# Softmax sums of A in row layout, reciprocals spread by DMA through DRAM, products on GpSimd

## Chip, cores, metric

One core of a Trainium2 chip. The metric is the device time of one launch in microseconds (us), median of the executions named. The kernel before takes 271.1 to 274.1 us in all rounds of this study.

## The reference, cut to what matters

```python
def sm(a, b):                                  # softmax over the last axis
    s = scale * a @ b.T; e = exp(s - max(s)); return e / (sum(e) + 1e-9)
A  = sm(q, k_lm)          # 576 rows x 32 landmarks, per batch (8) and head (8)
Bm = sm(q_lm, k_lm); C = sm(q_lm, k)
Z  = six Newton steps for the inverse of Bm
x  = A @ Z @ C @ v                             # then, over 4608 rows:
out = (sigmoid(x @ w_gate) * (x @ w_val)) @ w_out
```

## The kernel before

The exponentials of A (`aexp`) lie transposed: 128 partitions are four heads times 32 landmarks, the columns are the 576 rows, for two groups of heads. To normalise, each column wants a sum over the 32 partitions of its head, and the reciprocal must go back to those 32 partitions. The kernel folds Z, C, v and the gate weights into U and V, so the gate matmuls read the normalised A (`an`) directly.

```python
def norm(b):                                        # before, every batch
    for n in range(NB):                             # 10 matmuls with 4 columns
        for g in range(2):
            mm(out=sm[:, n, g, :], lhsT=aexp[:, g, blk0[n]:blk0[n] + 128], rhs=blk[:, :, 0])
    dve.reciprocal(out=ra, in_=sm_ra[:, 0])
    ...                                             # split into two bf16 parts, rhl
    tr(out=rt_ps, in_=rhl..., identity=ident)       # one transpose
    dve.tensor_copy(out=rt, in_=rt_ps)
    for g in range(2):
        for w, ns in ((0, (0, 1, 2)), (1, (3, 4))):
            for n in ns:                            # 10 matmuls: spread over 32 partitions
                mm(out=rb[...], lhsT=sel[...], rhs=rt[...])
            dve.tensor_mul(out=an[:, g, n0:n0 + nn], in0=aexp[:, g, n0:n0 + nn], in1=rb)

def ffn1(b):                                        # the gate step of batch b
    yield need(u_at, v_at - 0.24, an, banks=2)
    for g in range(2): mm(out=gp, lhsT=U[:, g, js], rhs=an[:, g, ws])
    for g in range(2): mm(out=vp, lhsT=V[:, g, js], rhs=an[:, g, ws])

def front(b):                                       # landmarks of batch b, b >= 3
    ...                                             # k and q transposed by DMA, summed on GpSimd
    pool.tensor_add(out=klm, ...); pool.tensor_add(out=bq[...], ...)
    yield made(mid_of, b - 1)
    load(b + 1, "v")                                # on GpSimd's DMA queue
```

One thing must be known for the rest. The order of all instructions is laid out when the program is built, by a **model** of the engines inside the kernel. `need(...)` holds a stream back until the model thinks its data have landed; other streams, output matmuls (op) above all, fill the time. On the chip every engine then works its list in order. Where the chip is later than the model, the engine stands.

The softmax here doesn't subtract the row's maximum and nothing guards it: scores larger than these inputs give would overflow.

Of the kernel before, what the change touches and what calls it, by code (L numbers as in the profile page):

```python
# [7 lines left out]
FP32 = mybir.dt.float32  # L8
BF16 = mybir.dt.bfloat16
# [11 lines left out]
class Model:  # L21
# [113 lines left out]
    def swap(self, src, dst):  # L135
# [3 lines left out]
        end = max(self.free["sp"], self.free["dma"]) + 2.5  # L139
        self.used[src.name] = self.used[dst.name] = self.landed[dst.name] = end  # L140


class Timed:

# [33 lines left out]
def kernel(ctx, tc, q, k, v, moe_w_gate, moe_w_val, moe_w_out, out):  # L178
# [12 lines left out]
    nc = tc.nc  # L191

    B, H, S, D = q.shape
# [3 lines left out]
    HF = S // 2  # L197
    NP = H // 2
# [9 lines left out]
    blk0 = [0, 128, 256, 384, S - 128]  # L208
    ITERS = 6

    DEFER = {"bs": 1.0, "sl": 1.0, "sa": 3.0, "cv": 0.5, "up": 0.0}
    LEAD, FIRST, ORDER = 100.0, (2,), ('k2', 'q2', 'o0', 'o1', 'o2', 'v2', 'k3', 'q3', 'v3')

    TURN, LATE = 3, 2
# [1 line left out]

    SWAP = 3

    consts = ctx.enter_context(tc.tile_pool(name="consts", bufs=1))
    wpool = ctx.enter_context(tc.tile_pool(name="wpool", bufs=1))  # L220
    keep = ctx.enter_context(tc.tile_pool(name="keep", bufs=1))
    sb = ctx.enter_context(tc.tile_pool(name="sb", bufs=2))
    ps = ctx.enter_context(tc.tile_pool(name="ps", bufs=3, space=bass.MemoryType.PSUM))
    ctx.enter_context(tc.manual_schedule())

    BANKS = 8
    model = Model(BANKS)
    act = Timed(nc.scalar, "act", model)
    dve = Timed(nc.vector, "dve", model)
    pool = Timed(nc.gpsimd, "pool", model)  # L230

    def bank(shape, dtype, name, hold=False):

        return model.take(ps.tile(shape, dtype, name=name, tag="p", bufs=BANKS), hold)
# [4 lines left out]
    def mm(slow=0.0, **kw):  # L239
        rhs, lhsT = kw["rhs"], kw["lhsT"]  # L240
        n = 1
        for x in rhs.shape[1:]:
            n *= x
        c = 1
        for x in lhsT.shape[1:]:
            c *= x
        nc.tensor.matmul(**kw)  # L247
        at = [x.start_partition() if hasattr(x, "start_partition") else 0 for x in (lhsT, kw["out"])]
        return model.pe(kw["out"], [lhsT, rhs], lhsT.shape[0], c, n, tuple(at), slow)

    def tr(**kw):
        nc.tensor.transpose(**kw)  # L252
        return model.pe(kw["out"], [kw["in_"]], kw["in_"].shape[0], 128, kw["in_"].shape[0])

    def need(*data, banks=0, tile=None):


        return data, banks, None if tile is None else DEFER[tile]

# [32 lines left out]
    def load_out(fc):  # L292
# [11 lines left out]
        out=ident, in_=ident, compare_op=ALU.not_equal, fill=1.0,  # L304
# [13 lines left out]
    for p in range(3):  # L318
# [4 lines left out]
        out=perm, in_=ident[0:P6, 0:P6].rearrange("p (l r) -> p r l", r=3))  # L323
# [3 lines left out]
        out=seg3, in_=ident[0:P6, 0:P6].rearrange("p (l r) -> p l r", r=3), axis=AX.X, op=ALU.max)  # L327
# [3 lines left out]
        out=comb, in0=ident[:, None, 0:64].to_broadcast([128, 2, 64]),  # L331
        in1=ident[:, None, 64:128].to_broadcast([128, 2, 64]))
# [8 lines left out]
        out=sel0, in0=ident[0:2 * NR, 0:NR], in1=ident[0:2 * NR, NR:2 * NR])  # L341

    blk0_ = consts.tile([128, NP], BF16, name="blk0")
    nc.vector.tensor_reduce(
        out=blk0_, in_=ident.rearrange("p (i l) -> p i l", l=m), axis=AX.X, op=ALU.max)
# [7 lines left out]
    front_of, sums_of, lm_of, value_of, mid_of, norm_of, an_of, uv_of, step_at = ({} for _ in range(9))  # L353
# [155 lines left out]
    def mid(b):  # L509
# [7 lines left out]
        bs = bank([128, 2, m], FP32, f"bs_{b}")  # L517
        for g in range(2):
            for i in range(NP):
                mm(  # L520
                    out=bs[32 * i:32 * i + 32, g, :], lhsT=bq[0:64, 2 * i + g, 0:m],
                    rhs=klm[0:64, 2 * i + g, :], start=True, stop=True,
# [47 lines left out]
        if b == 0:  # L570
            cs = bank([128, 2], FP32, f"cs_{b}", True)
            cv = [bank([128, D], FP32, f"cv_{b}{g}", True) for g in range(2)]
# [79 lines left out]
        spread(bd, Bc)  # L652


        aexp = sb.tile([128, 2, S], BF16, name=f"aexp_{b}", tag="aexp", bufs=2)

        def a_scores(g):
            for c, x in enumerate(row_scores("sa", g, klm, 0, qT)):
# [30 lines left out]
        if 0 < b < TURN:  # L689
            yield need(*cexp_at.values(), v_landed[0], banks=2)  # L690
            cs = bank([128, 2], FP32, f"cs_{b}")
            cv = bank([128, 2, D], FP32, f"cv_{b}")
            cv = [cv[:, g] for g in range(2)]
# [21 lines left out]
        if b >= TURN:  # L715
            value_of[b] = late_value

    def norm(b):

        aexp = norm_of.pop(b)  # L720
        yield need(aexp, banks=1)

        sm_ra = bank([128, 2, NR], FP32, f"sm_{b}")
        sm = sm_ra[:, 0].rearrange("p (n g i) -> p n g i", n=NB, g=2)
        for n in range(NB):
            for g in range(2):
                mm(
                    out=sm[:, n, g, :], lhsT=aexp[:, g, blk0[n]:blk0[n] + 128], rhs=blk[:, :, 0],
                    start=True, stop=True)
        ra = sm_ra[:, 1]  # L730
        dve.reciprocal(out=ra, in_=sm_ra[:, 0])
        rhl = sb.tile([128, 2, NR], BF16, name=f"rhl_{b}", tag="rhl")
        dve.tensor_copy(out=rhl[:, 0, :], in_=ra)
        dve.tensor_sub(out=rhl[:, 1, :], in0=ra, in1=rhl[:, 0, :])
        yield need(rhl, banks=1)
        rt_ps = bank([2 * NR, 128], BF16, f"rtp_{b}")
        tr(out=rt_ps, in_=rhl.rearrange("p s r -> p (s r)"), identity=ident)
        rt = sb.tile([2 * NR, 128], BF16, name=f"rt_{b}", tag="rt")
        dve.tensor_copy(out=rt, in_=rt_ps)
        an = sb.tile([128, 2, S], BF16, name=f"an_{b}", tag="an", bufs=3)  # L740
        for g in range(2):
            for w, ns in ((0, (0, 1, 2)), (1, (3, 4))):
                yield need(rt, banks=1)
                n0 = 384 * w
                nn = min(S, n0 + 384) - n0
                rb = bank([128, nn], FP32, f"rb_{b}_{g}{w}")
                for n in ns:
                    lo = 64 if n == 4 else 0
                    o = blk0[n] + lo - n0
                    mm(  # L750
                        out=rb[:, o:o + 128 - lo],
                        lhsT=sel[:, (2 * n + g) * NP:(2 * n + g + 1) * NP, :],
                        rhs=rt[:, lo:128], start=(n == ns[0]), stop=(n == ns[-1]))
                dve.tensor_mul(
                    out=an[:, g, n0:n0 + nn], in0=aexp[:, g, n0:n0 + nn], in1=rb)
        an_of[b] = an
# [15 lines left out]
    def advance_by(b, g, out, lhs, rhs, name, twice=False):  # L772

        p = bank([128, rhs.shape[1]], FP32, name)
        mm(out=p, lhsT=minus2, rhs=rhs, start=True, stop=False)
        mm(out=p, lhsT=lhs, rhs=rhs, start=False, stop=True)
        return each(b, g).mul(out, p[:, None, :].to_broadcast([128, 2, D]) if twice else p, -1.0)

    def first_newton(b):
        y, bd, at = mid_of[b]  # L780
        y = y[:, :, 128:128 + D]
        for it in range(ITERS):
            last = it == ITERS - 1
            n = sb.tile([128, 2, 2, D] if last else [128, 2, D], BF16, name=f"y_{b}_{it + 1}", tag=f"y{last}", bufs=2)
            model.by_part.add(n.name)
            new = []
            for g in range(2):
                yield lambda: 0.0 if len(square_of[b]) > it else None
                S, s_at = square_of[b][it]
                yield need(at[g], s_at[g], banks=1)  # L790
                new.append(advance_by(b, g, n[:, g], S[:, g, 0:128], y[:, g], f"py_{b}_{it}{g}", last))
            y, at = n, new
        return y, at
# [215 lines left out]
    def mids():  # L1009
        for b in range(B):  # L1010
            yield made(lm_of, b)
            if b > 2:
                yield step(b - 2)
            yield from mid(b)

    def norms():
        for b in range(B):
            yield made(norm_of, b)
            yield from norm(b)
# [126 lines left out]
```

## Time and profile before

| | before |
|---|---|
| median of 3 | 271.84 us |
| span of the profile | 269.7 us |
| TensorE, VectorE, ScalarE, GpSimd busy | 260.1, 193.3, 159.4, 96.2 us |
| TensorE clock granted | 0.998 |

The span runs from the first to the last instruction and stands about 2 us under the time. TensorE is the engine that bounds; the lines are in the prediction. Here is what the prediction doesn't show and the argument needs: SyncE's queue, the one that carries output, transposes and small exchanges, in the timeline of the kernel before (start, length, queue, line, operation, out<-in, count).

```profile
138.25 1.12 SPq L480 DMA_DIRECT2D s_5q<-s_5q  x2
144.38 0.79 SPq L959 DMA_DIRECT2D out_dram<-ob  x2
149.04 1.33 SPq L384 DMA_TRANSPOSE ct<-cl  x1
```

It is busy here and there, in order, and nothing in it is waited for by the gate step.

### The profile page before, as it was taken

The numbers are of one execution on the slowest core, as the hardware profiler recorded it, in microseconds if no ns is written. First come the engines' busy times: TensorE is split into PE (matmuls) and PEld (weight loads), VectorE is DVE, ScalarE is ACT, GpSimd is POOL, SyncE is SP. The second block draws the span as 40 slices with busy tenths as digits, with TensorE's granted clock in tenths as the row PEclk, the third lists the DMA queues.
The fourth block names the chain that finished last, engine by engine and source line by source line (L and its number), as shares of the span: only waits on it lengthen the run. The fifth ranks groups of instructions, "written<-read, shape, count | busy, mean of one in ns | idle before, by whom it ended". The sixth has DMA issues, their size and how long they took to land.

```text
span 269.7 us, 8019 instructions
## 1 busy us (share of the span) xinstructions
PE 260.1 (96%) x3089; PEld 167.0 (62%) x3123; DVE 193.3 (72%) x551; ACT 159.4 (59%) x413; POOL 96.2 (36%) x107
## 2 busy tenths in 40 slices
PE   8999999999999999999999999999999999999994
PEld 5877777757664666556646665556636664665443
DVE  4566888976899788948986778848968786963111
ACT  3663876866647754876477655875368643964001
POOL 8523231960874039511953078212922000000000
PEclk9999999999999999999999999999999999999999
DMA  6999999999795998889794989589530413101433
GB/s 94 193 206 205 205 206 206 205 203 172 141 194 115 204 170 121 181 135 199 141 221 72 182 157 203 129 139 199 124 90 12 97 41 80 41 0 41 117 103 92
DMA packets 62645, 38.00 MB, mean 141 GB/s; under 512 B 33552, under 2 KB 58128, under 8 KB 62608
## 3 DMA queue, kind: packets, MB, share of 16 engines
q0 software_dynamic: 23600, 18.88, 47.0%
q1 hardware_dynamic: 38896, 18.52, 31.4%
q8 instruction: 24, 0.39, 0.6%
q14 instruction: 13, 0.11, 0.1%
q10 hardware_dynamic: 112, 0.10, 0.1%
HBM read 37.75 MB, written 9.44 MB: 175 GB/s over the span
## 4 chain that ended last, share of the span: by engine, by line
PE 93%; ACT 2%; issue 2%; POOL 1%; DVE 0%; POOLq 0%; ACTq 0%
PE op L247 34%; PE gp L247 18%; PE vp L247 18%; PE idle_ps L247 3%; PE pn L247 2%; PE cv L247 2%; PE rb L247 2%; PE sc L247 1%; PE sa L247 1%; PE tp_q L252 1%; PE up_1g L247 1%; PE up_0g L247 1%; PE up_2g L247 1%; PE tp_k L252 1%; PE up_1v L247 1%
## 5 line engine op out<-in xcount | busy, mean ns | idle before, releaser
L247 PE MATMUL op<-wo_sb,ht 128*128 128x512 bf16 (+1 forms) x410 | 109.4, 373 | 2.1 <-issue 1.1
L153 ACT ACTIVATE th<-gp 128x288 bf16<-128x288 f32 x192 | 76.7, 415 | 48.4 <-PE gp L247 36.7
L153 DVE SCALAR_TENSOR_TENSOR ht<-th,vp 128x288 bf16<-128x288 bf16 x192 | 82.0, 448 | 21.9 <-ACT th L153 17.2
L247 PE MATMUL gp<-an,U 128*128 128x288 bf16 x384 | 78.5, 286 | 0.3
L247 PE MATMUL vp<-an,V 128*128 128x288 bf16 x384 | 78.4, 286 | 0.0
L247 PEld LDWEIGHTS <-ht 128*128 128x128 bf16 x444 | 39.9, 98 | 26.7 <-issue 5.8
L247 PEld LDWEIGHTS <-U 128*128 128x128 bf16 x384 | 35.9, 98 | 27.3 <-issue 2.5
L247 PEld LDWEIGHTS <-V 128*128 128x128 bf16 x384 | 37.5, 98 | 9.7 <-issue 0.2
L153 ACT ACTIVATE ob<-op 128x512 f32<-128x512 f32 (+1 forms) x31 | 18.2, 587 | 29.6 <-PE op L247 24.2
L153 DVE SCALAR_TENSOR_TENSOR sy<-sy,pn 128x384 bf16<-128x384 bf16 x35 | 19.2, 548 | 2.3 <-PE pn L247 1.9
L153 DVE TENSOR_SCALAR ob<-op 128x512 f32<-128x512 f32 (+2 forms) x7 | 4.2, 596 | 17.3 <-PE op L247 17.3
L247 PE MATMUL idle_ps<-idle_w 128*128 128x256 bf16 x86 | 14.8, 308 | 1.2 <-DVE idle_w L297 1.2
L247 PE MATMUL pn<-sy 128*128 128x192 bf16 (+1 forms) x84 | 13.1, 237 | 0.4 <-ACT kT L153 0.3
L153 DVE TENSOR_TENSOR an<-aexp,rb 128x384 bf16<-128x384 bf16 (+1 forms) x32 | 12.4, 446 | 0.3 <-PE rb L247 0.3
L247 PEld LDWEIGHTS <-sy 128*128 128x128 bf16 x88 | 8.1, 97 | 6.2 <-DVE sy L153 2.8
L153 ACT ACTIVATE aexp<-sa 128x288 bf16<-128x288 f32 x32 | 10.7, 418 | 1.5 <-PE sa L247 1.1
L247 PEld LDWEIGHTS <-idle_w 128*128 128x128 bf16 x86 | 8.5, 109 | 3.3 <-DVE idle_w L297 1.2
L247 PEld LDWEIGHTS <-WT 64*32 64x32 bf16 x384 | 3.8, 89 | 9.1 <-issue 6.6
L270 POOL DMA_DIRECT2D kn<-in_k_dram x9 | 7.0, 779 | 4.6 <-DMA wg_sb<-in_moe_w_gate_dram 2.1
L153 DVE CAST U<-up_0g 128x512 bf16<-128x512 f32 x8 | 5.5, 690 | 4.1 <-PE up_0g L247 4.1
L270 POOL DMA_DIRECT2D vn<-in_v_dram x8 | 6.3, 789 | 5.3 <-PE gp L247 4.5
L270 POOL DMA_DIRECT2D qn<-in_q_dram x9 | 6.8, 753 | 4.0 <-PE sm L247 2.2
(201 smaller groups left out, 349.7 us busy)
## 6 DMA issues: line engine op xcount, KB each, us to landing
vn<-in_v_dram POOLq DMA_DIRECT2D x8, 576.0 KB, 9.4
kn<-in_k_dram POOLq DMA_DIRECT2D x7, 576.0 KB, 8.1
qn<-in_q_dram POOLq DMA_DIRECT2D x7, 576.0 KB, 10.6
out_dram<-ob SPq DMA_DIRECT2D x53, 64.0 KB, 3.0
out_dram<-ob SPq DMA_DIRECT2D x17, 192.0 KB, 2.3
out_dram<-ob SPq DMA_DIRECT2D x18, 128.0 KB, 2.4
wg_sb<-in_moe_w_gate_dram POOLq DMA_DIRECT2D x3, 512.0 KB, 19.7
wv_sb<-in_moe_w_val_dram POOLq DMA_DIRECT2D x3, 512.0 KB, 21.0
```

The lines of the kernel that those rows point to most:

```text
L153: f(**kw)
L247: nc.tensor.matmul(**kw)
L252: nc.tensor.transpose(**kw)
L270: nc.gpsimd.dma_start(out=t[:, hs], in_=src[b, hs].rearrange("h (p c) d -> p h (c d)", p=P6))
```

## The change

The intent: take the 21 small matmuls of the normalisation off TensorE and the products off VectorE. The sums come out in row layout (8 matmuls on 128x32 tiles), the reciprocals go out to DRAM and come back spread over 32 partitions each, and GpSimd, which idles, multiplies in place. Batches 2 to 7. Cut to its core:

```diff
+    def widen(self, src, dst, n=1):                 # what the model assumes of such a transfer
+        start = max(self.free["pe"], self.free["sp"], self.landed.get(src.name, 0.0), ...)
+        self.free["sp"] = start + 0.55 * n
+        self.free["dma"] = max(self.free["dma"], start) + 0.5 * n
+        end = max(self.free["dma"], self.free["sp"]) + 2.0
...
-        aexp = sb.tile([128, 2, S], BF16, name=f"aexp_{b}", tag="aexp", bufs=2)
+        aexp = sb.tile([128, 2, S], BF16, name=f"aexp_{b}", tag="aexp", bufs=3)
...
+    def wide_norm(b, aexp):
+        for c in range(2):
+            for j in range(4):
+                mm(out=sm[32 * j:32 * j + 32, :], lhsT=pairs[0][:, c], rhs=aexp[:, j // 2, o:o + QT], ...)
+        for x in range(2):
+            at = dve.reciprocal(out=ra[:, half], in_=sm[:, half])
+        far = away.tile([2, 2, NP, 4, HF], FP32, ...)               # in DRAM
+        nc.sync.dma_start(out=far..., in_=ra)
+        model.widen(ra, far)
+        yield need(far)
+        for i in range(NP):
+            nc.sync.dma_start(out=wide[32 * i:32 * i + 32], in_=far[:, :, i, 0]....partition_broadcast(32))
+        model.widen(far, wide, NP)
+        for j in range(4):
+            yield need(wide)
+            part = aexp[:, j // 2, (j % 2) * HF:(j % 2 + 1) * HF]
+            pool.tensor_mul(out=part, in0=part, in1=wide[:, j])
+        an_of[b] = aexp
...
-        an = sb.tile([128, 2, S], BF16, name=f"an_{b}", tag="an", bufs=3)
+        an = aexp                                                    # batches 0 and 1, old way, in place
```

More of the change, by code (lines that the diff above doesn't have):

```diff
@@ L140, in swap @@
         self.used[src.name] = self.used[dst.name] = self.landed[dst.name] = end
+    def widen(self, src, dst, n=1):
+        start = max(self.free["pe"], self.free["sp"], self.landed.get(src.name, 0.0),
+                    self.waits.get(dst.name, 0.0))
+        self.free["sp"] = start + 0.55 * n
+        self.free["dma"] = max(self.free["dma"], start) + 0.5 * n
+        end = max(self.free["dma"], self.free["sp"]) + 2.0
+        self.used[src.name] = self.used[dst.name] = self.landed[dst.name] = end
 class Timed:
@@ L209 @@
     ITERS = 6
-    DEFER = {"bs": 1.0, "sl": 1.0, "sa": 3.0, "cv": 0.5, "up": 0.0}
+    DEFER = {"bs": 1.0, "sl": 1.0, "sa": 3.0, "cv": 0.5, "up": 0.0, "sm": 1.0}
     LEAD, FIRST, ORDER = 100.0, (2,), ('k2', 'q2', 'o0', 'o1', 'o2', 'v2', 'k3', 'q3', 'v3')
@@ L217 @@
     SWAP = 3
+    WIDE, QT, pairs = 2, S // 4, []
     consts = ctx.enter_context(tc.tile_pool(name="consts", bufs=1))
@@ L222 @@
     sb = ctx.enter_context(tc.tile_pool(name="sb", bufs=2))
+    away = ctx.enter_context(tc.tile_pool(name="away", bufs=1, space=bass.MemoryType.DRAM))
     ps = ctx.enter_context(tc.tile_pool(name="ps", bufs=3, space=bass.MemoryType.PSUM))
@@ L716, in mid @@
             value_of[b] = late_value
+    def wide_norm(b, aexp):
+        if b == WIDE:
+            pairs.append(consts.tile([128, 2, 32], BF16, name="pairs"))
+            nc.vector.memset(pairs[0], 0.0)
+            to = pairs[0].rearrange("p c (i u d) -> p c i u d", u=4, d=2)
+            for c in range(2):
+                dve.tensor_copy(out=to[:, c, :, :, c], in_=blk0_[:, :, None].to_broadcast([128, NP, 4]))
+        yield need(aexp, banks=1, tile='sm')
+        sm = bank([128, QT], FP32, f"sm_{b}")
+        for c in range(2):
+            for j in range(4):
+                o = (j % 2) * HF + c * QT
+                mm(
+                    out=sm[32 * j:32 * j + 32, :], lhsT=pairs[0][:, c],
+                    rhs=aexp[:, j // 2, o:o + QT], start=(c == 0), stop=(c == 1))
+        ra = sb.tile([128, QT], FP32, name=f"ra_{b}", tag="ra", bufs=1)
+        for x in range(2):
+            half = slice(x * QT // 2, (x + 1) * QT // 2)
+            at = dve.reciprocal(out=ra[:, half], in_=sm[:, half])
+            yield need(at + (0.3 if x == 0 else 0.0))
+        far = away.tile([2, 2, NP, 4, HF], FP32, name=f"far_{b}", tag="far", bufs=2)
+        nc.sync.dma_start(out=far.rearrange("g w i u (c x) -> (g w i u c) x", c=2), in_=ra)
+        model.widen(ra, far)
+        yield need(far)
+        wide = sb.tile([128, 4, HF], FP32, name=f"rw_{b}", tag="rw", bufs=1)
+        for i in range(NP):
+            nc.sync.dma_start(
+                out=wide[32 * i:32 * i + 32],
+                in_=far[:, :, i, 0].rearrange("g w x -> (g w) x").partition_broadcast(32))
+        model.widen(far, wide, NP)
[4 more added lines that the diff above has]
+        an_of[b] = aexp
     def norm(b):
         aexp = norm_of.pop(b)
+        if b >= WIDE:
+            yield from wide_norm(b, aexp)
+            return
         yield need(aexp, banks=1)
@@ L783, in first_newton @@
             last = it == ITERS - 1
-            n = sb.tile([128, 2, 2, D] if last else [128, 2, D], BF16, name=f"y_{b}_{it + 1}", tag=f"y{last}", bufs=2)
+            n = sb.tile([128, 2, 2, D] if last else [128, 2, D], BF16, name=f"y_{b}_{it + 1}", tag=f"y{last}", bufs=1 if last else 2)
             model.by_part.add(n.name)
```

## The prediction

> **What bounds the kernel now.** I read the page first, then the busy time of each engine by stretch, then the chain of work that ended last, then the groups and tiles that the change touches, and last the timeline of GpSimd and of the SyncE queue.
>
> From the page of the kernel before, busy times, slices and the chain:
>
> ```profile
> PE 260.1 (96%) x3089; PEld 167.0 (62%) x3123; DVE 193.3 (72%) x551; ACT 159.4 (59%) x413; POOL 96.2 (36%) x107
> PE   8999999999999999999999999999999999999994
> PE 93%; ACT 2%; issue 2%; POOL 1%; DVE 0%; POOLq 0%; ACTq 0%
> ```
>
> TensorE is busy 96% of the span, and the chain that ended last runs through it for 93%. From 34 to 246 us the table by stretch says how little is left over (columns: window, length, then busy time of PE, weight load, VectorE, ScalarE, GpSimd, then clock, DMA share, GB/s):
>
> ```profile
> 34.00:246.00 212.00, 209.05 (x2377) 132.18 (x2407) 167.95 (x460) 136.45 (x357) 81.42 (x83) 1.00 0.78 140
> ```
>
> 212.00 - 209.05 = 2.95 us of TensorE idle time in that stretch. So what this change can give is TensorE time that it takes away, plus at most those 3 us.
>
> What the softmax normalisation of A costs TensorE is read from the chain of work between 126.5 and 132.5 us, batch 4 (start, length, what):
>
> ```profile
> 127.47 0.17 PE pn L247 x2
> 127.63 0.25 PE sm L247 x10
> 127.88 0.45 PE op L247 x2
> ...
> 128.99 0.43 PE op L247 x2
> 129.42 0.06 PE rtp L252
> 129.47 0.24 PE gp L247 x2
> ...
> 130.56 0.52 PE rb L247 x10
> 131.07 0.43 PE op L247 x2
> ```
>
> Everything is packed end to end, so these lengths are what the next instruction waited: 0.25 us for ten sums, 0.06 for one transpose, 0.52 for ten broadcasts of the reciprocals, 0.83 us a batch. The durations of single instructions (0.17 to 0.23 us) overlap and must not be summed. VectorE's share is in the groups:
>
> ```profile
> L153 DVE TENSOR_TENSOR an<-aexp,rb 128x384 bf16<-128x384 bf16 (+1 forms) x32 | 12.4, 446 | 0.3 <-PE rb L247 0.3
> L153 DVE RECIPROCAL sm<-sm 128x40 f32<-128x40 f32 x8 | 3.3, 409 | 0.0
> L153 POOL TENSOR_TENSOR s_5k<-kT 128x768 f32<-128x768 bf16 x1 | 1.6, 1643 | 11.3 <-DMA kT<-kn 11.3
> ```
>
> The third line is GpSimd: it waited 11.3 us for the transposed k of batch 5 at 126.92 us, then its timeline is full of landmark sums until 144 us. The normalisation of batch 4 falls exactly there.
>
> **What the Trainium skill says.** "TensorEngine Tiling (Array Packing)", Key Properties: tiles work in parallel, but changing the tiling mode drains the array. The trace agrees: 16 score matmuls (sa, 64x32 tiles, two rounds of 288 columns, 0.24 us at 2.4 columns per ns) hold the chain 0.37 us, so 0.13 us for the change, and a gap of 0.16 us follows at 126.44. "GPSIMD Engine Reference", Elementwise: a two-input operation takes about 2.6 cycles an element at 1.2 GHz; 768 elements took 1.643 us here, 2.57 cycles, so it agrees. "DMA: Bandwidth & Descriptors", Anatomy of one DMA: about 2 us of fixed cost, mostly waiting for the write receipt. The 64 KB exchanges of batch 7, with no loads about, land in 2.0 us; those of batches 3 to 6 for k, beside loads, in 5.6 to 6.2. So agreement on an empty queue only. "SBUF — State Buffer", Who interferes with whom: VectorE operations with two SBUF inputs hold up GpSimd's reads. The gate (th, vp) and the Newton step have one input in PSUM; the gate takes 396 to 455 ns all through the run, with GpSimd busy or not, so I expect little of this.
>
> **The change part by part**, for one batch of the six (2 to 7).
>
> TensorE, removed: 0.25 + 0.06 + 0.52 = 0.83 us. Added: eight matmuls of 128x32 tiles with 144 columns, four side by side, two rounds: 2 x 144 / 2.4 = 0.12 us, plus 0.13 to 0.29 us for the change of mode in and out (from sa above), less where the scheduler sets it beside other tiled work. I take 0.30. Net 0.53 us, all on the bounding engine: 6 x 0.53 = 3.2 us.
>
> VectorE, removed: reciprocal 0.41, two halves of the bf16 split 2 x 0.20, copy of the transpose 0.21, four products 4 x 0.446 = 1.78; sum 2.80 us. Added: two reciprocals of 72 columns. From 166 ns for 2 columns and 409 for 40, 6.4 ns a column: 0.166 + 70 x 0.0064 = 0.61 us each, 1.22 us. Net 1.6 us a batch, 9.5 us in all, but VectorE has 44 us to spare in the 212: beside other work. It can shorten only TensorE's waits on it, which are some 5 us of weight-load waits and under 3 us of idle. I count 0.3 us.
>
> GpSimd, added: four products of 288 elements at 2.57 cycles, 0.62 plus some 0.05 us each: 2.7 us a batch, 16 us in all, on an engine idle 64% of the time. Beside other work if its place in the queue is right.
>
> DMA, added: 73 KB out to DRAM, then four reads that write 147 KB each: 0.66 MB a batch, 4 MB on 38. It is not bandwidth but latency that counts. Before: first sum at 127.47, last product done at 132.76, 5.3 us. After: 0.3 for the matmuls, 0.2 to VectorE, 1.2 reciprocals, 2.5 to 5.5 for the write, 3 to 6 for the reads, 2.7 for the products: 10 us on an empty queue, 16 beside loads. The step that uses it, the first gate matmul of batch 4, comes 0.4 us after the last up matmul (139.9 us), 12.8 us after the first sum. So in batches 3 to 6 that step moves by up to 3 us, some more if the schedule, which is laid out from a model that puts a transfer behind all loads queued, thinks it later.
>
> Does that cost? Not at once: TensorE has other work. At the start of the eight gate steps I counted output matmuls (op) done against those whose input exists: at batches 3 to 6 some 55 to 64 are in reserve, 12 to 14 us at 0.216 us each. They fill a late step; batch 7, which ends the run, has no loads beside it (10 to 11 us, in time).
>
> Sum: 269.7 - 3.2 - 0.3 = 266.2 us of span; I give back 0.6 us for stalls where the schedule's guess of a landing is wrong. 266.8 of span, and the measured time stands 2.1 us above the span (271.84 against 269.7): 268.9 us, 1.1% faster.
>
> **The rivals.** First, **GpSimd's order**. The chain that paces the batches is: k transposed by DMA, GpSimd sums (126.92 to 144.3), landmark scores, softmax of C, its transpose (149.04), next k transposed (150.47, landed 156.6): 29.7 us a round, and the later gate steps start right when their weights are up (230.25 and 230.58). If the four products sit in GpSimd's queue before the landmark products bq (142.81), each round grows by 2.7 us or by the wait for the read as well. Five rounds: 14 us, of which the reserve hides some 8: about +5 us, so 274 to 275. For it: in-order queue, busy window. Against it: all sums of the next batch are issued before the products, and the reads land late enough to fall behind bq, where GpSimd idles over 10 us. Chance 0.15.
>
> Second, **a late operand becomes a TensorE stall**: writing, then reading through DRAM takes longer than the schedule thinks, and TensorE, in order, stands. One microsecond for each of five batches takes away 5 us: 271 to 274. For it: the spread of 2.0 to 6.2 us for the same exchange. Against it: the products come 10 us before most uses of that data end, and a schedule that assumes FIFO behind loads errs on the safe side. Chance 0.2.
>
> Third, **VectorE relief counts**: with six fewer PSUM banks asked for and 1.6 us less VectorE work a batch, most of the 3 us of idle goes too: 266 us. Chance 0.1.
>
> **Range and chances.** The main line gives 268 to 270; the third rival sets the low end, 266.2, the second the high end, 273.0. More than 2% faster means below 266.4, which needs all of the 0.83 us saved with nothing added, or the third rival in full: 0.08. More than 2% slower means above 277.3, the first rival beyond my estimate: 0.06. The rest, 0.86, is within 2%.
>
> **What would show it.** Right: sm, rtp and rb for batches 2 to 7 replaced by eight matmuls that hold the chain 0.25 to 0.4 us; TensorE busy near 257 us; VectorE down by about 9 us; GpSimd up by about 16; products ending 10 to 16 us after the sums; GpSimd's sums of the next k still 29 to 30 us apart; output matmuls moved ahead of the gate steps of batches 3 to 6. Wrong: TensorE idle between 34 and 246 us clearly above 3 us, with gate matmuls waiting for GpSimd; bq waiting behind the products; or output transfers held in the SyncE queue behind a read that waits for its write, with ScalarE waiting for its output buffers. The last matters as well if it lengthens the chain of k.

## The result

| | before | after |
|---|---|---|
| first chip, median of 4 | 272.16 us | 283.51 us (279.09 to 290.68) |
| ratio of fast runs, 95% interval | 1 | 1.028 (1.022 to 1.035) |
| another chip, 4 runs (again) | 272.91 us | 290.60 us; ratio 1.062 |
| a third set, 6 runs (again2) | 272.01 us | 288.63 us; ratio 1.054 |
| TensorE clock of the runs | 0.991 to 1.0 | 0.958 to 0.994 |

A ratio is the mean time of one kernel's fast runs over that of the other's of the same rounds, so not quite the ratio of the medians. Outputs are correct. The change is 3 to 6% slower, and it is unsteady: its executions differ by up to 4%. "Fast" is said within one call: the two fast runs of the first chip took 279.09 and 280.63 us at a clock of 0.994 and 0.992, while all four of again have 0.958 to 0.970 and would have counted as slow beside them. Those two faster executions were not profiled. The first profile of the change fell in the slow state, so I read the one of the run again, a fast one of its call. From its page, the busy times, slices of TensorE, and the clock, in tenths:

```profile
PE 265.7 (92%) x3014; PEld 164.7 (57%) x3046; DVE 189.6 (66%) x521; ACT 159.7 (55%) x410; POOL 112.9 (39%) x131
PE   8899999999966999999995899976999999989994
PEclk9999999999999799999999599996999999999999
```

TensorE has fewer instructions, yet is busy 5.6 us longer, in a span of 289.2 us; and the slices fall to 5 or 6 tenths where they were 9. The clock falls in or just after those slices. Who TensorE waits for is in its view of waits (us in total, times, longest):

```profile
PE gp L259 <- POOL aexp L162: 11.7, 7, 3.2
```

The chain of work in batch 4 shows one such stop whole (start, length, what):

```profile
132.55 0.13 PE sm L259 x8
132.68 0.35 PE gp L259 x2
...
145.81 0.22 PE up_2v L259 x8
146.02 0.35 PE gp L259 x2
...
149.47 0.42 SPq L757
...
150.91 7.16 DMA rw<-far
...
158.93 1.43 POOL aexp L162 x2
160.40 0.40 PE gp L259
160.79 0.48 PE vp L259 x2
161.27 0.21 PE s L259 x2
161.49 0.48 PE gp L259 x2
```

Three things are to be seen. The new sums cost TensorE 0.13 us, less than I thought. The reads of the reciprocals are issued at 149.47, 17 us after the sums, and one of them takes 7.16 us of the chain; the gate step, whose weight matmuls end at 146.03, starts its first matmul at 159.02, after a stop of 3.17 us, and its second at 160.4, after 1.10 us more. And from then on two gate matmuls take 0.48 us where they took 0.24: the clock is half. The Trainium skill, "TensorE: Matmul & The Clock Gate" (Part 1, What's actually happening), gives 1.2 GHz as the state "after ≥1 idle window (~3.4µs)". The case agrees on the half clock (granted 0.5), but not on a whole idle window: in batch 2 it fell to half behind stops of 1.48 and 1.10 us with a matmul between them. Three such stretches, behind batches 2, 4 and 5, last 3.4, 6.8 and 6.8 us, 17.1 us in all. Before the stop TensorE did have other work, as I had counted on, but it was used up. SyncE's queue and GpSimd in the same stretch:

```profile
137.01 0.54 SPq L752 DMA_DIRECT2D far<-ra  x1
144.76 1.11 SPq L492 DMA_DIRECT2D s_5q<-s_5q  x2
148.63 0.79 SPq L1011 DMA_DIRECT2D out_dram<-ob  x2
149.47 1.88 SPq L757 DMA_DIRECT2D rw<-far  x4
```
```profile
149.92 0.79 POOL L282 DMA_DIRECT2D vn<-in_v_dram  x1
158.23 2.80 POOL L162 TENSOR_TENSOR aexp<-aexp,rw 128x288 bf16<-128x288 bf16 x4 [7.52 <-DMA rw<-far]
```

The write lands in under 6 us (4.7 in batch 4), but the reads are issued 12.5 us after its issue, and the next v (576 KB) is loaded beside them. The reads stand in SyncE's queue behind an output transfer (148.63) that itself waited for its tile. All six batches of that run, from the same views (us; a read's time is from its issue to its landing):

| batch | sums | reads issued | v load issued | reads land in | first product | TensorE stops |
|---|---|---|---|---|---|---|
| 2 | 73.3 | 85.6 | 86.4 | 2.6 to 4.4 | 91.6 | 1.5 + 1.1 |
| 3 | 104.5 | 117.8 | 120.2 | 2.7 to 3.1 | 122.7 | none |
| 4 | 132.4 | 149.5 | 149.9 | 3.0 to 7.2 | 158.2 | 3.2 + 1.1 |
| 5 | 169.3 | 186.1 | 185.8 | 6.4 to 7.7 | 195.4 | 2.9 + 1.1 |
| 6 | 206.7 | 214.7 | none | 3.1 to 3.6 | 219.9 | none |
| 7 | 239.3 | 246.0 | none | 3.0 to 3.7 | 251.9 | 0.9 |

The kernel's own model can be printed while the order is laid out; for batch 4 of the changed kernel it believes:

```
sums 124.36   write landed 139.94   reads issued 140.02   reads landed 144.22
products done 147.41   gate step 147.51      end of the program: 261.23 (kernel before: 263.94)
```

From the sums on, the model issues the reads at +15.7 and ends the products at +23.1; the chip issues them at +17.1 and ends the products at 161.0, +28.7. The model's end of the program is 2.7 us earlier than that of the kernel before: it made the same forecast as I did, from the same error.

### The profile page after: what moved, and what is told of

Its sections match the earlier page's. It is cut to its first block, busy times and chain, and to the rows that moved or that the text cites. A ratio compares the mean times of both kernels' runs of the same rounds, so it can differ in the third digit from the quotient of the medians.

```text
span 288.8 us, 7934 instructions
## 1 busy us (share of the span) xinstructions
PE 265.0 (92%) x3014; PEld 163.8 (57%) x3046; DVE 188.2 (65%) x521; ACT 160.0 (55%) x410; POOL 112.8 (39%) x131
## 4 chain that ended last, share of the span: by engine, by line
PE 75%; DMA 11%; SPq 3%; POOL 3%; issue 3%; ACT 2%; DVE 1%; POOLq 1%; ACTq 0%; DVEq 0%
PE op L259 24%; PE gp L259 17%; PE vp L259 16%; DMA rw<-far 7%; PE idle_ps L259 2%; PE pn L259 2%; DMA s_3k<-s_3k 2%; POOL aexp L162 2%; DMA kn<-in_k_dram 2%; SPq L1011 2%; PE cv L259 2%; SPq L757 1%; PE sc L259 1%; PE sa L259 1%; PE tp_q L264 1%
## 5 line engine op out<-in xcount | busy, mean ns | idle before, releaser
L259 PE MATMUL op<-wo_sb,ht 128*128 128x512 bf16 (+1 forms) x412 | 104.1, 377 | 2.0 <-issue 1.2
L259 PE MATMUL gp<-aexp,U 128*128 128x288 bf16 x384 | 81.7, 294 | 12.8 <-POOL aexp L162 12.3
L259 PE MATMUL vp<-aexp,V 128*128 128x288 bf16 x384 | 80.8, 293 | 0.0
L259 PEld LDWEIGHTS <-ht 128*128 128x128 bf16 x444 | 40.8, 98 | 38.7 <-issue 7.9
L259 PEld LDWEIGHTS <-V 128*128 128x128 bf16 x384 | 38.4, 100 | 15.6 <-issue 4.9
L162 POOL TENSOR_TENSOR aexp<-aexp,rw 128x288 bf16<-128x288 bf16 x24 | 16.8, 730 | 61.8 <-DMA rw<-far 32.7
L162 ACT ACTIVATE ob<-op 128x512 f32<-128x512 f32 (+1 forms) x27 | 15.8, 586 | 32.8 <-PE op L259 29.2
L162 DVE TENSOR_SCALAR ob<-op 128x512 f32<-128x512 f32 (+2 forms) x11 | 6.9, 631 | 32.6 <-PE op L259 30.3
L162 DVE TENSOR_SCALAR sy<-s,rc 128x128 bf16<-128x128 f32 x15 | 4.6, 345 | 10.0 <-PE s L259 9.7
L162 ACT ACTIVATE cl<-sl 128x288 bf16<-128x288 f32 x20 | 8.0, 411 | 1.8 <-PE sl L259 1.7
```

The lines of the kernel that those rows point to most:

```text
L162: f(**kw)
L259: nc.tensor.matmul(**kw)
```

## The experiments

**Theory L**, after seeing the profile: the operand is late, TensorE stops, its clock falls. **Rivals**: G, the place of the products on GpSimd delays the landmark sums and so the pace of the batches; B, in-place work and the buffer counts; T, the traffic by itself.

### again: the changed kernel once more

No edit.

> The changed kernel once more, on the chip of the next three runs. Theory L (late operand: the reciprocals come back from DRAM about 5 us after the schedule expects them, TensorE stands at the first gate matmul, and its clock falls after the stop): 279 to 291 us, TensorE idle several us ahead of the first gate matmul of most of batches 2 to 7, released by the GpSimd products. Theory G (order on GpSimd: the four products delay the landmark sums, so each round of the chain that paces the batches grows): the same time. Theory B (working in place, three buffers for the exponentials): the same time.

290.60 us, ratio 1.062 (1.055 to 1.068). It is the profile read above.

### notrip: no transfers, constant reciprocals

Wrong on purpose, though by little, as the sums of 32 small exponentials are all near 32.

```diff
-        far = ...; nc.sync.dma_start(out=far..., in_=ra); yield need(far)
-        wide = ...; four reads
-            yield need(wide)
-            pool.tensor_mul(out=part, in0=part, in1=wide[:, j])
+            yield need(ra)
+            pool.tensor_mul(out=part, in0=part, in1=flat)     # a tile of 1/32
```

> Wrong on purpose: the products take a constant 1/32 instead of the reciprocals, and the two transfers are gone; sums, reciprocals and the four GpSimd products stay. L: no late operand, so the saved TensorE time shows: 0.70 us a batch as the chain has it (0.83 less 0.13), 4.2 us in all, 267 to 269 us, no stop of TensorE above 1 us after batch 1. G: the products still stand in the GpSimd queue, still 276 us or more. B: still 276 us or more.

270.92 us, ratio 0.994 (0.989 to 0.999). From its page:

```profile
PE 257.9 (96%) x3014; PEld 161.9 (60%) x3046; DVE 187.8 (70%) x518; ACT 160.4 (60%) x414; POOL 112.7 (42%) x131
PE   8999999999997999999999999999999999999994
PEclk9999999999999999999999999999999999999999
```

Same instructions on TensorE (3014), same products on GpSimd (112.7 us busy), and both the stops at the gate step and the clock loss are gone. With the wait for the transfers goes 19.7 us of time against again, which includes what the low clock took there. G and B predicted 276 us or more and fall. For G this is a hard test: without the wait the products of batch 4 stand at 138.81 in GpSimd's queue, ahead of klm and bq, the very place that the first rival feared. But 270.9 is above my 267 to 269.

### unread: the transfers made, but nobody waits

```diff
-            yield need(wide)
-            pool.tensor_mul(out=part, in0=part, in1=wide[:, j])
+            yield need(ra)
+            pool.tensor_mul(out=part, in0=part, in1=flat)
```

> Wrong on purpose: as the run before, but both transfers are made as in the changed kernel, into a tile that nobody reads. It asks what the traffic and the place in the SyncE queue cost by themselves. L: at most 1 us more than without the transfers, 267 to 270 us. A rival, theory T (the 4 MB more of traffic, or the SyncE queue held up, slows the transposes and the output): 273 us or more, with a longer time from the issue of the k transposes to their landing, or ScalarE and VectorE waiting for output buffers.

272.01 us, ratio 0.995 (0.990 to 1.000). From its page:

```profile
PE 258.2 (96%) x3014; PEld 162.2 (60%) x3046; DVE 189.5 (70%) x518; ACT 160.3 (59%) x414; POOL 112.7 (42%) x131
```

It is 1.1 us more than without the transfers, within the noise: so little the traffic and the places in SyncE's queue cost when nobody waits. T falls. In this run as in notrip the order laid out changes too, since the model no longer holds the gate step back: the difference to again is that of the whole late operand, planned wait and unplanned stop together. Against this page TensorE in again is 7.5 us longer busy (265.7), with the same instructions. My figure of at most 270 was missed by 2 us, by the same amount as the run before.

### wide8: old normalisation, new buffers

```diff
-    WIDE, QT, pairs = 2, S // 4, []
+    WIDE, QT, pairs = 8, S // 4, []
```

> The old normalisation in all eight batches, but in place and with the buffer counts of the changed kernel. L, G and T: as before, 271 to 273 us. B: 276 us or more.

274.53 us, ratio 1.005 (1.000 to 1.010). So the buffers (one of them, for the last Newton step, went from two to one) and the order that follows from them cost half a per cent, hardly clear of noise. That would explain the two misses above: against this run, which differs from notrip in the normalisation and the order laid out for it, the saving is 274.53 - 270.92 = 3.6 us, for the 4.2 us expected.

### told5: the model is told that the reads land later

```diff
-        end = max(self.free["dma"], self.free["sp"]) + 2.0
+        end = max(self.free["dma"], self.free["sp"]) + (7.0 if n > 1 else 2.0)
```

> The kernel's work unchanged, but the model from which its order is laid out is told that the reads land 5 us later, which is what the trace shows. My prediction's claim was that other matmuls fill a late step, some 12 us of them in reserve. If so, TensorE gets other work in place of the stops: 272 to 278 us. If the reserve is too small (the model itself ends 24 us later then, at 285 against 261), the time is as bad as the changed kernel or worse: 285 to 295 us.

293.99 us, ratio 1.082 (1.077 to 1.087). Knowing of the delay doesn't hide it. The model, printed in the same way, itself stood for 4.5, 5.3 and 2.1 us from 97.8 on, with 9 output tiles done of the 9 whose input existed: the reserve was empty. On the chip the order came out worse still. GpSimd's timeline:

```profile
107.95 1.48 POOL L162 TENSOR_TENSOR s_4q<-s_4q 128x256 f32<-128x256 f32 x2
109.39 2.81 POOL L162 TENSOR_TENSOR aexp<-aexp,rw 128x288 bf16<-128x288 bf16 x4
```

Those are the products of batch 2, whose reads were issued at 84.5: they got behind the whole block of landmark sums, and TensorE stood 7.4 us for them. So the run mixes an empty reserve with rival G, which the changed kernel itself doesn't show.

### vlate: the load of v after the products

```diff
                 yield made(mid_of, b - 1)
+                yield made(normed, b - 1)        # set once the products of b - 1 are in the queue
                 load(b + 1, "v")
```

> The load of the next v, which the changed kernel puts into the DMA queues just ahead of or beside the four reads of the reciprocals, is issued after the products instead. In the profile of the run again the reads landed in 2.7 to 3.1 us in batch 3 (v issued after them) and 3.5 in batch 6 (no v), and in up to 7.2 and 6.4 to 7.7 us in batches 4 and 5 (v just ahead). Theory V (that load makes the read late): reads of batches 4 and 5 land within 3.5 us, the stops there, 4.3 and 4.0 us, shrink to under 1 us, and with the half clock after them gone the time falls by 8 to 11 us, to 278 to 282. Rival (the wait is the round trip itself and the order in the SyncE queue): reads stay at 5 us or more, time as the changed kernel, 286 to 292.

279.11 us, ratio 1.026 (1.021 to 1.030): as expected, 11.5 us less than again. That difference holds both the shorter stops and the clock, which in this profile never falls to half after the start. It is also measured against a call of slow-clocked executions: the two fast runs of the unchanged program on the first chip, 279.09 and 280.63 us, are no slower than vlate. Each view of the reads below is of one batch, 4 and then 5, first of again and then of vlate:

```profile
DMA to landing us min/median/max: 3.0/4.2/7.2
DMA to landing us min/median/max: 6.4/7.1/7.7
```
```profile
DMA to landing us min/median/max: 2.8/3.1/3.3
DMA to landing us min/median/max: 3.1/3.4/3.6
```

The products of batch 4 begin 4.9 us after the first read is issued instead of 8.8:

```profile
149.44 1.84 SPq L758 DMA_DIRECT2D rw<-far  x4
154.31 2.81 POOL L162 TENSOR_TENSOR aexp<-aexp,rw 128x288 bf16<-128x288 bf16 x4 [2.48 <-DMA rw<-far]
```

The Trainium skill, "DMA: Bandwidth & Descriptors", Issuing engines are not separate DMA queues, says that transfers from all queues run on the same 16 DMA engines and interleave. This pair of runs agrees and adds the size: a 144 KB read lands in 2.7 to 3.6 us, and in up to 7.7 with one 576 KB load issued just before or among the reads. Stops of 1.1 to 1.9 us are left in four batches.

### warm: dummy matmuls over the stops

```diff
             gp = bank([128, HF], FP32, f"gp_{b}_{j}{w}")
+            for _ in range({2: 30, 4: 40, 5: 40, 7: 14}.get(b, 0) if w == 0 and j == 0 else 0):
+                nc.tensor.matmul(out=gp[:, 0:256], lhsT=idle_w[:, 0:128], rhs=idle_w, start=True, stop=True)
```

> The changed kernel with dummy matmuls (256 columns, into the bank of the first gate matmul, which overwrites them) ahead of the first gate matmul of batches 2, 4, 5 and 7: 30, 40, 40 and 14, 0.107 us each, about as long as the stops. The operand is as late as ever; only the clock is kept up. Theory C (much of the loss is the half clock that follows a stop: TensorE busy 265.7 us in the run again against 258.2 with unread transfers, 7.5 us): the time falls by 5 to 8 us, to 282 to 286, with the clock at 0.99 or above. Rival (the stop alone costs): no change or, where dummies outlast the stop, a longer time: 289 to 293.

287.78 us, ratio 1.056 (1.048 to 1.064), the clock 0.992 to 1.0 in all four runs. TensorE's timeline at batch 4:

```profile
155.63 4.53 PE L948 MATMUL gp<-idle_w 128*128 128x256 bf16 x40
160.00 0.29 PE L259 MATMUL gp<-aexp,U 128*128 128x288 bf16 x1
160.74 0.28 PE L259 MATMUL gp<-aexp,U 128*128 128x288 bf16 x1 [0.46 <-POOL aexp L162]
160.86 0.41 PE L259 MATMUL vp<-aexp,V 128*128 128x288 bf16 x2
```

The operand comes no sooner (160.7 against 160.4), the clock stays up, and the time, 2.8 us under again (an earlier call on the same chip), falls by less than the intervals. So filling the stops keeps the clock up, and in this pair the low clock isn't most of the loss. Theory C's 5 to 8 us aren't there.

### again2 and warm2: the same pair in one call, five rounds

warm2 has 52 dummies at batch 2 instead of 30.

> The changed kernel, beside the next two runs. 280 to 292 us, clock 0.96 to 0.99.

> The changed kernel with dummy matmuls over the stops, 52 in place of 30 at batch 2 (its stop there was 2.5 us longer than the dummies). The operand is as late as ever. Theory C (the half clock after a stop is a cost of its own): the clock stays at 0.99 or above, and the time is 3 to 8 us under the changed kernel of the same rounds. Rival (only the stop costs, or the half clock falls into waits that are there anyway): within 1.5 us of it.

again2: 288.63 us, ratio 1.054 (1.050 to 1.058). warm2: 288.15 us, ratio 1.061 (1.057 to 1.065), clock 0.993 to 1.0. No gain, though warm2's dummies outlast the stops in this execution (at batch 2 they run until 97.5, the products are there at 92.3), so what a full clock gives and what the dummies take can't be parted. How much of the loss is the half clock stays open. An upper bound can be estimated: 17.1 us at half clock in again can have cost at most half of that, 8.5 us, and the pages show 7.5 us of longer busy time.

### halves: products shared by VectorE and GpSimd

With the v load after the products:

```diff
-        for j in range(4):
+        for j in (0, 2, 1, 3):                   # first half of the columns of both groups first
-            pool.tensor_mul(...)
+            (pool if j % 2 else dve).tensor_mul(...)
```

> The v load after the products, and the products in the order in which the gate step needs them: the two of the first half of the columns on VectorE, the two of the second half on GpSimd. It should bring the first gate matmuls a further 1.5 to 2 us forward. If lateness is all: no stop above 1 us from batch 3 on, and the time comes to 269 to 274 us, about the kernel before or 1% better. If something else costs, it stays near the run with the v load moved alone.

283.48 us, ratio 1.040 (1.035 to 1.045): a miss, slower than vlate. The stops at the gate step do shrink, but the order laid out is another one, and TensorE now waits mostly elsewhere:

```profile
PE cv L259 <- DMA ct<-cl: 5.6, 3, 2.1
PE gp L259 <- DVE aexp L162: 1.4, 3, 0.6
```

The transposed C comes by DMA too, and now its reader is laid out too early for it.

### vorder: vlate with the products reordered, all on GpSimd

```diff
-        for j in range(4):
+        for j in (0, 2, 1, 3):
```

> The v load after the products (279.1 us in its own run, 1.026 of the kernel before), and the four GpSimd products in the order in which the gate step needs them: the first half of the columns of both groups first. The laid-out order of every engine but for these four instructions is the same. TensorE stops twice at the start of a batch now, the second time 1.10 us for the third product; with the new order the second stop falls to about 0.4 us, in five batches 3 to 4 us: 275 to 277 us, ratio 1.010 to 1.016. If the remaining loss is not lateness: 1.022 or more.

> The v load after the products, products reordered, once more. If lateness is what remains and the half clock is not triggered: 275 to 278 us, ratio 1.010 to 1.018. If the half clock comes and goes by execution, as in the first run of it: a spread of over 5 us, with time and clock moving together.

On one chip 280.51 us, six runs from 276.5 (clock 0.991) to 287.3 (0.975), ratio of the fast ones 1.033 (1.027 to 1.038). On another (vorder2) 277.40 us, ratio 1.021 (1.017 to 1.025): five runs of 276.4 to 279.4 at clock 0.999 to 1.0, and one of 293.2 at 0.965. The second stop fell from 1.1 to 0.4 us as expected, and the better runs are in the range expected; by ratio both calls missed it, and the first lies where I had put "the remaining loss is not lateness". Against vlate the median is 1.4 us worse on the one chip and 1.7 us better on the other. And one program, unchanged, takes 277 us at a clock of 1.0 and 293 at 0.965; what makes it fall in one execution and not in the next isn't shown.

### vtwo: two of the four reads on ScalarE's queue

On top of vorder's edit:

```diff
-            nc.sync.dma_start(out=wide[...], in_=far[...])
+            (nc.scalar if i % 2 else nc.sync).dma_start(out=wide[...], in_=far[...])
```

> As the run with the products reordered, and two of the four reads go out from ScalarE's queue instead of SyncE's, so the last read is issued about 0.9 us earlier (four issues take 1.87 us on one queue). If lateness is all: another 0.5 to 0.9 us less at each remaining stop, 273 to 276 us, ratio 1.003 to 1.014, and never below the 1.0 or so of the kernel with unread transfers. If ScalarE's own queue holds the reads up, or the issues cost ScalarE time that TensorE needs: as with the products reordered, or longer.

285.24 us, ratio 1.036 (1.030 to 1.043), slower, with waits of 3.2 and 2.0 us for the transposed C (ct) in its profile and the clock at 0.976 to 0.985. No gain from a shorter issue; why the wait moved to ct I didn't follow up.

### only367: the new way in batches 3, 6 and 7

On top of vorder's edit:

```diff
-        if b >= WIDE:
+        if b in (3, 6, 7):
             yield from wide_norm(b, aexp)
```

> The new normalisation in batches 3, 6 and 7 only, those whose reads had no v load ahead of them, with the products reordered; the old one, in place, in the others. Three batches save 0.70 us of TensorE each, 2.1 us on the 274.5 of the old normalisation with these buffers: 272 to 274 us, ratio 0.998 to 1.005, if batches with a late operand are what made the rest slow. If a late operand anywhere upsets the order of the batches after it: 276 us or more.

275.34 us, ratio 1.008 (1.001 to 1.014): 1.3 us over the range, and under the 276 of the other reading, so it decides nothing. No version of the change beat the kernel before. The bound is near: with no wait for the transfers at all, notrip was 0.6% faster.

## Why the prediction was wrong, point by point

The prediction, 268.9 us with 266.2 to 273.0, was wrong: 3 to 6% slower. The second rival, a late operand turned into a TensorE stall, was the one that came true; I gave it 0.2 and sized it at 271 to 274.

- **TensorE's saving**: right in kind, too small in size. The eight sums hold the chain 0.13 us, not 0.30, in batches 4 to 7, where they come right behind other tiled work (cv), and 0.24 in batches 2 and 3, where they don't; so 0.70 or 0.59 us a batch instead of 0.53. The saving is real: 3.6 us between wide8 and notrip.
- **VectorE and GpSimd**: a reciprocal of 72 columns took 0.60 us (0.61 predicted), a GpSimd product 0.73 us (0.67). GpSimd's busy time rose by 16.7 us (16). VectorE's fell by 3.7 us, not 9: it also took 11 output evictions instead of 7 (6.9 against 4.2 us) and 1.1 us to set up the tile for the sums, and the four old products, which overlap, had held it 1.54 us a batch (131.22 to 132.76), not 1.78.
- **Latency of the round trip: the step that failed.** I put it at 10 to 16 us from the first sum to the last product. Batch 4 needed 28.7: 4.6 until the write was issued (1.7 in my sum), 4.7 until it landed (2.5 to 5.5), 7.8 more until the reads were issued (not in my sum), 8.8 from there to the first product (3 to 6) and 2.8 for the products (2.7). Batches 6 and 7, with no loads about, needed 16.0 and 15.4; batches 2 and 3 needed 21, batch 5 28.9. The largest part isn't transfer: the reads were issued 12.5 us after the write's issue, because the model puts a transfer behind all loads queued and lays out the reads only when it thinks the write has landed (139.94, 15.6 us after the sums). I had named that very assumption and written that it errs on the safe side. It is safe for the model's own waits, but it makes the transfer late in fact, and it places the reads beside the next v load, which cost another 4 us. vlate takes away that second part: 11.5 us of time against again, the clock's share included. What the first part costs was not tested: no run issues the reads as soon as the write has landed.
- **"They fill a late step"**: they did, until they ran out. In batch 4 the work in reserve covered the time from 147.5 to about 155.8, with 35 output matmuls where I had counted 55 to 64; then TensorE stood. told5 says that a schedule that knows of the delay runs out as well.
- **The term for stalls**: 0.6 us. Measured, the stops at the gate steps sum to 11.7 us in the run again, (1.5 + 1.1) + (3.2 + 1.1) + (2.9 + 1.1) + 0.9. Between again and unread lie 18.6 us.
- **Not in the prediction**: the clock. Stops are followed by stretches of matmuls of double length, and executions of one program differ by up to 6%. The length of a stop alone doesn't decide it: in the profile of vorder the clock fell to half at 85.3 us, after waits of 1.08 and 0.53 us, and in that of unread it stayed up after 2.06 and 0.45. Its share of the loss isn't settled.
- **The first rival** (GpSimd's order) didn't happen in the changed kernel: the products came after bq, as I argued. Nor did it cost what I feared where it did happen: in notrip and unread they stand ahead of bq in batch 4, and both runs are fast. The sign that I named, sums of the next k 29 to 30 us apart, failed all the same (29.8, 34.4, 30.3 and 37.1 us in again).
- **Two readings**: the gap of 0.16 us at 126.44 follows the tiled matmuls cv, not the scores sa; and the 2 us of fixed cost are stated under "Anatomy of one DMA" for transfers that GpSimd issues, while the exchanges here are SyncE's.
- **The buffers**: that three buffers in place would cost anything wasn't considered; wide8 has them at +0.5%, hardly clear of noise.

## What to carry to other kernels

A saving on the bounding engine is worth nothing when the data it produces go a longer way to their next use: compare the whole way with the time to the use, from the instant when the first instruction can issue, including queue order and whatever is loaded beside it. An in-order engine pays in full for what a static schedule guesses too early, and on TensorE stops of 1 to 3 us were often followed by a slower clock on top. Before building such a path, run it with the operand replaced by a constant: that one run shows about the most that the change can give, here 0.6%.

## What the Trainium skill lacked or had wrong

- "DMA: Bandwidth & Descriptors" (Issuing engines are not separate DMA queues; Latency and other measured facts): it says that queues interleave, with no figure for a small transfer beside a large load. Here a 144 KB read landed in 2.7 to 3.6 us, and in 6.4 to 7.7 us with one 576 KB load issued 0.4 us ahead from another queue.
- The same page has no figure for a write to DRAM that is read back. Here a write of 72 KB landed in 1.6 to 5.5 us.
- "TensorEngine Tiling (Array Packing)", Key Properties: a change of tiling mode drains the array, with no cost beside it. Eight matmuls on 128x32 tiles held the chain 0.13 us behind 96x32 ones and 0.24 us behind full ones, of which 0.12 are their columns at 2.4 per ns; the pair of full matmuls after them took 0.35 us instead of 0.24.
- "GPSIMD Engine Reference", Elementwise: the 2.6 cycles an element hold for 768 elements (1.64 us); at 288 elements a product took 0.730 us, 3.0 cycles an element. A fixed part of some 0.1 us would account for it (an estimate; the types differ too).
- "TensorE: Matmul & The Clock Gate" has no figure for how much of a window must be idle before the clock falls. Here it fell behind two waits that add up to 1.6 us (vorder) and to 2.6 us (again, batch 2), and stayed up behind two that add up to 2.5 us (unread).
